# A one-core kernel with a written order: w_out in four transfers, in-place GpSimd additions, and a new order of all its steps

## The chip, the cores and the metric

The kernel runs on one NeuronCore of a Trainium2 chip. The metric is the device time of one execution in microseconds (us), as the median of several runs. A profile of one execution stands beside it; its times are counted from the start of its span, and the span is shorter than the device time by what lies around it.

The engines are named as the profile names them: PE is the matrix engine, PEld its weight loads, DVE the vector engine, ACT the scalar engine, POOL is GpSimd, and SP is the engine that issues nearly all transfers here.

## The reference

Two blocks follow each other. Attention has no softmax: queries and keys go through a sketch, and the values are gathered once per head.

```python
# q, k, v: (4, 4, 1088, 32); S1, S2: (8, 32), float64
a = einsum('rd,bhsd->bhsr', S1, x); b = einsum('rd,bhsd->bhsr', S2, x)
phi(x) = einsum('bhsi,bhsj->bhsij', a, b).reshape(..., 64)
kv = einsum('bhsf,bhsd->bhfd', phi(k), v);  z = sum(phi(k), axis=2)
x = (phi(q) @ kv) / (phi(q) @ z + 1e-6)        # back to (4352, 128)
# w1, w2: (128, 1024); w3: (1024, 1024); w_out: (1024, 128), float64
out = ((x @ w1) * (x @ w2)) @ w3 @ w_out       # (4352, 128)
```

The arithmetic is float32 on the chip. S1, S2 and the four weights arrive as float64, so the kernel reads their words as integers and builds float32 from them.

## The kernel before, in words

**Steps and their order.** All work is cut into 952 named steps. A step issues one or a few instructions, mostly on one engine. The string `ORDER` lists all of them, and the kernel calls them in that order (L1527); instructions of one engine are chained in it (L1530 to L1534), so `ORDER` fixes what each engine, and the queue of SP, does after what. An engine that waits holds back all that stands behind it. `SLOTS` fixes which buffer each tile takes, `POOL` and `ACTS` say which of the elementwise steps run on GpSimd or ACT rather than on DVE. The order was worked out outside the kernel; in the kernel it is a constant.

**Key side, one batch b of four.** `k{b}.load` and `k{b}.loadr` bring keys, `k{b}.max` and `k{b}.g` find their size, `k{b}.lead` and `k{b}.rest` split them in a leading and a small part, and `k{b}.gram0` to `gram4` (L604) multiply keys with keys in 144 small matmul passes of 32 columns by 128 rows. `Gm` to `Ts` and `N0`, `N1` shape the denominator; `ab`, `kp`, `kv0` to `kv3`, `kvr` and `kq` build phi(k) and kv.

**Query side.** `q0` to `q4`, `q6` and `qr` are seven groups of tokens, which fill the nine token tiles of the next block. In each, `tr`, `max`, `l2`, `l1`, `rm` split the queries, `A0`, `C0`, `C1` (L1294) project them, a run of DVE and GpSimd steps from `sm` to `phi` forms phi(q), `pT` turns it, and `x` (L1408) and `xT` (L1419) give the token tile of the next block.

**The feed-forward part.** For each token tile g (0 to 7 of 512 tokens, r of 256) and each of eight column blocks c there are five steps: `g{g}.{c}a` and `b` (L1448, L1458), one float32 matmul of two passes each; `c`, a copy by ACT (L1453); `m`, the product by DVE (L1464); and `o` (L1471), which accumulates the output. `w3` and `w_out` are multiplied into one matrix first: `f{n}.t` transposes a chunk of w3 on DVE (L472), and `f{n}.m` multiplies it with w_out in 16 passes on PE (L478).

**Weights.** `w0` and `w1` carry w1 and w2, `w2` carries w_out, `w3` to `w10` the eight chunks of w3. Each has a load, two readings of its words on ACT (`c` L229, `m` L417), a shift on DVE (`j` L431) and two integer additions on POOL (`a0`, `a1`). w_out comes in one transfer in which partition p holds rows 8p to 8p+7 (L396). The rows of w_out and the columns of w3 must be in one order, so for w3 the shift writes back into its own input and the two additions write the permuted order into another tile (L439 to L442).

**Fillers.** `warm0` to `warm28` are 72 matmuls on zeros whose results nobody reads (L221). They keep PE active in the places that the order gives them; there are as many of them after the change as before.

A step's *tile shape* is the part of the PE array that its passes use: 128x128 for the feed-forward part, 128x32, 64x32 or 32x32 for most of the attention part.

## Time and profile before

The median is 254.46 us of three runs (254.37 to 256.15). The profiled execution took 254.37 us; its span is 252.6 us, so 1.8 us lie around it. The granted clock of PE is 1.00 in all the stages below. PE works from 1.0 to 249.4 us; the first feed-forward matmul, `g0.3a`, starts at 30.3 us. The busy times are those of the profile's stage view, in us.

| Stage, us | PE | DVE | ACT | POOL | mean DMA share |
|---|---|---|---|---|---|
| 0 to 30.3, start | 28.02 | 24.43 | 19.21 | 15.43 | 0.71 |
| 30.3 to 60 | 29.67 | 27.25 | 21.34 | 14.81 | 0.88 |
| 60 to 95 | 35.00 | 33.52 | 21.50 | 14.91 | 0.72 |
| 95 to 120 | 24.01 | 17.05 | 7.27 | 9.45 | 0.08 |
| 120 to 165 | 45.00 | 30.56 | 14.64 | 10.51 | 0.01 |
| 165 to 249.4 | 84.40 | 26.92 | 15.78 | 1.71 | 0.16 |
| 249.4 to 252.6, tail | 0.01 | 0.29 | 0.00 | 0.00 | 0.20 |

Matmuls overlap in their pipeline, so a PE that is busy throughout can still lose time between two groups: then the next group starts later after the one before it than the passes alone need. That is read from the start times in the timeline, and not from the busy time.

### The profile page before, as it was taken

How to read it: one execution, taken by the hardware profiler on the slowest of the kernel's cores; microseconds unless marked ns; L12 is line 12 of the kernel's file. 1: busy time of each engine (PE TensorE's matmuls, PEld its weight loads, DVE VectorE, ACT ScalarE, POOL GpSimd, SP SyncE). 2: the span in 40 equal slices, each digit the busy share in tenths (PEclk: the TensorE clock that was granted, in tenths of full speed). 3: DMA queues.
4: the chain of work that ended last, by engine and by line, in shares of the span. 5: the costliest groups of instructions: out<-in, count | busy, mean ns of one | idle time of the engine just before them, and what ended most of it. 6: DMA issues, size and time to landing. Idle time of an engine off the chain costs nothing.

```text
span 252.6 us, 5980 instructions
## 1 busy us (share of the span) xinstructions
PE 246.1 (97%) x2503; PEld 137.9 (55%) x2503; DVE 160.0 (63%) x358; ACT 99.7 (39%) x183; POOL 66.8 (26%) x99
## 2 busy tenths in 40 slices
PE   8799999999999999998999999999999999999994
PEld 6689845457456576456446444444444444456554
DVE  2999998989998995938677597550115371424040
ACT  4588398763918543340225143213340012211010
POOL 4644535393546309203540016010000001000000
PEclk9999999999999999999999999999999999999999
DMA  6867793996679930200000000000000007205014
GB/s 182 262 173 263 222 241 84 259 254 139 160 206 235 249 90 0 85 6 3 3 0 3 3 0 1 4 0 0 3 0 0 0 2 123 44 0 83 0 28 76
DMA packets 31130, 22.01 MB, mean 87 GB/s; under 512 B 21248, under 2 KB 25600, under 8 KB 30976
## 3 DMA queue, kind: packets, MB, share of 16 engines
q1 hardware_dynamic: 30416, 21.05, 33.9%
q10 hardware_dynamic: 688, 0.59, 0.7%
q8 instruction: 19, 0.31, 0.5%
q14 instruction: 7, 0.06, 0.1%
HBM read 19.40 MB, written 2.23 MB: 86 GB/s over the span
## 4 chain that ended last, share of the span: by engine, by line
PE 95%; issue 1%; DMA 1%; POOL 1%; ACT 1%; DVE 0%; SPq 0%; POOLq 0%; ACTq 0%
PE a_ps L1448 23%; PE b_ps L1458 23%; PE ps_o L1471 22%; PE ps_w3o L478 6%; PE ps_g L604 3%; PE ps_x L1408 2%; PE idle_ps L221 2%; PE ps_ac L1294 2%; PE ps_kv L714 2%; PE ps_or L1478 1%; DMA s_raw<-in_S_dram 1%; PE ps_ab L672 1%; PE ps_ab L647 1%; PE ps_xt L1195 1%; PE ps_kt L630 1%
## 5 line engine op out<-in xcount | busy, mean ns | idle before, releaser
L1464 DVE TENSOR_TENSOR ab<-ffa,b_ps 128x512 f32<-128x512 f32 (+1 forms) x72 | 44.9, 649 | 60.8 <-PE b_ps L1458 40.9
L1453 ACT COPY ffa<-a_ps 128x512 f32<-128x512 f32 (+1 forms) x72 | 38.6, 566 | 96.4 <-PE a_ps L1448 93.8
L1448 PE MATMUL a_ps<-xT,w 128*128 128x512 f32 (+1 forms) x144 | 66.7, 570 | 0.0
L1458 PE MATMUL b_ps<-xT,w 128*128 128x512 f32 (+1 forms) x144 | 65.5, 569 | 0.0
L1471 PE MATMUL ps_o<-ab,w3o 128*128 128x512 f32 x128 | 62.3, 594 | 0.0
L1448 PEld LDWEIGHTS a_ps<-xT,w 128*128 128x128 f32 x144 | 26.5, 190 | 30.0 <-issue 23.9
L1458 PEld LDWEIGHTS b_ps<-xT,w 128*128 128x128 f32 x144 | 26.9, 190 | 29.1 <-issue 25.0
L1471 PEld LDWEIGHTS ps_o<-ab,w3o 128*128 128x128 f32 x128 | 23.9, 190 | 25.5 <-issue 24.0
L442 POOL TENSOR_TENSOR w3c<-cv_c,cv_m 128x512 int32<-128x512 int32 x16 | 20.8, 1333 | 22.0 <-DVE cv_c L431 13.7
L1389 POOL TENSOR_TENSOR ph<-s_al,s_bs 128x1024 f32<-128x1024 f32 (+1 forms) x6 | 10.8, 1808 | 52.7 <-DVE s_bs L1379 52.7
L478 PEld LDWEIGHTS ps_w3o<-wo,w3T 128*128 128x128 f32 x128 | 15.4, 192 | 3.6 <-issue 3.3
L478 PE MATMUL ps_w3o<-wo,w3T 128*128 128x128 f32 x128 | 15.6, 275 | 0.0
L221 PE MATMUL idle_ps<-zeros 128*128 128x256 bf16 x72 | 13.3, 317 | 1.0 <-DVE zeros L193 1.0
L229 ACT ACTIVATE cv_c<-raw 128x1024 f32<-128x1024 f32 x11 | 12.8, 1175 | 2.1 <-DMA raw<-in_moe_w_dram 2.1
L417 ACT ACTIVATE cv_m<-raw 128x1024 int32<-128x1024 uint32 x11 | 12.8, 1178 | 0.0
L472 DVE STREAM_TRANSPOSE w3T<-w3c 128x1024 f32<-128x1024 f32 x8 | 9.8, 1230 | 3.5 <-POOL w3c L442 3.5
L604 PE MATMUL ps_g<-kk 128*32 128x64 f32 x288 | 8.2, 225 | 2.1 <-POOL kk L596 1.1
L1346 POOL TENSOR_TENSOR s_al<-s_hl 128x128 f32<-128x128 f32 (+2 forms) x3 | 2.3, 753 | 29.7 <-DVE s_hl L1341 29.7
L1419 ACT COPY xT<-ps_x 128x128 f32<-128x128 f32 (+2 forms) x20 | 4.6, 325 | 13.1 <-PE ps_x L1408 9.5
L1397 DVE STREAM_TRANSPOSE pT<-ph 128x1024 f32<-128x1024 f32 (+1 forms) x7 | 8.2, 1164 | 2.5 <-POOL ph L1389 2.4
L221 PEld LDWEIGHTS <-zeros 128*128 128x128 bf16 x72 | 7.5, 114 | 3.9 <-issue 1.0
L604 PEld LDWEIGHTS ps_g<-kk 128*32 128x32 f32 x288 | 7.0, 109 | 2.8 <-POOL kk L596 1.2
(241 smaller groups left out, 284.3 us busy)
## 6 DMA issues: line engine op xcount, KB each, us to landing
raw<-in_moe_w_dram SPq DMA_DIRECT2D x32, 256.0 KB, 7.6
qh<-in_q_dram SPq DMA_DIRECT2D x4, 544.0 KB, 3.5
out_dram<-oT SPq DMA_DIRECT2D x33, 64.0 KB, 2.0
raw<-in_moe_w_dram SPq DMA_DIRECT2D x4, 512.0 KB, 5.8
k<-in_k_dram SPq DMA_DIRECT2D x3, 512.0 KB, 5.9
v<-in_v_dram SPq DMA_DIRECT2D x2, 512.0 KB, 6.4
raw<-in_moe_w_out_dram SPq DMA_DIRECT2D x1, 1024.0 KB, 6.0
kh<-in_k_dram SPq DMA_DIRECT2D x8, 128.0 KB, 6.3
```

The costliest lines, as they stand in the source:

```text
L221: pe.matmul(t, zeros, bview(zeros, [[0, 2], [1, 128]]), start=True, stop=True)
L229: act.activation(dst, hi.bitcast(F32), ACT.Prelu, scale=2.0 ** -112, alpha=-2.0 ** 32)
L417: act.mul(x["m"], words(0).bitcast(U32), 2.0 ** -29)
L442: pool.tensor_tensor(d, c, m, ALU.add)
L478: pe.matmul(t["o"], w3T[ko][:, c], wo[:, c], start=c == 0, stop=c == NC - 1)
L604: pe.matmul(o[h * D:(h + 1) * D], lhs, rhs, start=start, stop=stop, skip_group_check=True)
L1389: on(nm(f"phi{u}")).tensor_mul(x, bview(s["al"][:, u * g], [[r, g], [1, r], [0, r]]), bview(s["bs"][:, u * g], [[r, g], [0, r], [1, r]]))
L1448: pe.matmul(x["a"][:, :w], w_of(0, c), xT[g][:, c0:c0 + w], start=True, stop=True)
L1453: act.copy(x["s"][:, :w], x["a"][:, :w])
L1458: pe.matmul(x["b"][:, :w], w_of(1, c), xT[g][:, c0:c0 + w], start=True, stop=True)
L1464: dve.tensor_mul(ab_sb[g, c][:, c0:c0 + w], x["s"][:, :w], x["b"][:, :w])
L1471: pe.matmul(o_ps[g], w3o[:, c], ab_sb[g, c], start=c == 0, stop=c == NC - 1)
```

## The change

There are three edits; the third is by far the largest.

```diff
 w2.load:
-  sp.dma_start(raw[n], bass.AP(w_out, ap=[[NC * DM, 128], [1, NC * DM]]))
+  for t in QUARTERS:                       # 0, 2, 1, 3
+      sp.dma_start(raw[n][t * 32:(t + 1) * 32],
+                   bass.AP(w_out, offset + t * 256 * DM, ap=[[DM, 32], [32 * DM, NC], [1, DM]]))
 w{n}.j:
-  d = x["c"].bitcast(I32) if 3 <= n and n - 3 not in BY_PE else made()
-  on(f"w{n}.j").tensor_scalar(d, x["c"].bitcast(I32), 3, None, ALU.logical_shift_left)
+  on(f"w{n}.j").tensor_scalar(made(), x["c"].bitcast(I32), 3, None, ALU.logical_shift_left)
 w{n}.a0, a1:
-  if 3 <= n and n - 3 not in BY_PE:
-      (d, c, m as views with the two inner axes of d exchanged)
-      pool.tensor_tensor(d, c, m, ALU.add)
-      return
   d = x["d"].bitcast(I32)[:, i * 512:(i + 1) * 512]
   pool.tensor_tensor(d, d, x["m"][:, i * 512:(i + 1) * 512], ALU.add)
```

w_out now comes in four transfers of 32 partitions, each row of 1 KB on its own, so that partition p of part t holds rows 256t + 32c + p. With that, the columns of w3 need no permutation: the shift writes straight into the tile of the result, and both additions work in place and contiguously.

`ORDER`, `SLOTS`, `POOL` and `ACTS` are all replaced. The same 952 steps remain, with the same 2503 PE passes, so a step only moves. What the moves amount to, counted in the two orders:

- 25 elementwise steps change engine. From POOL to DVE: `s.low`, `s.sum`, `k0.rest0`, `s.blkh`, `q1.al`, `q1.p2`, `k1.kp1`, `q2.al`, `q4.phi0`, `q4.phi1`, `q6.p12`, `q6.phi1`, `qr.al`, `qr.p2`, `qr.phi0`. From DVE to POOL: `k0.kp1`, `q0.al`, `k0.Nf`, `k1.kp0`, `q3.p12`, `k3.rest0`, `q6.al`, `qr.p12`. From ACT to DVE: `s.lead`, `k3.lead0`.
- SP issues `k0.loadr` ahead of `s.load` (before: behind it). `c.act`, a copy of one element that came first on ACT, now stands far behind, after `g2.1c`.
- From `g0.3a` on, two neighbouring PE steps differ in tile shape in 42 places (before: 46), and 7 filler matmuls stand there (before: 10).
- `k2.kv0` to `kvr` and `k3.gram0` to `gram4`, which followed each other with `k3.ab` between them (232 passes), are now apart: the 144 passes of `k3.gram` come first, then seven feed-forward steps and a filler, then the 72 of `k2.kv`. `k2.gram0` to `gram4`, which had feed-forward and other steps close to them and `q1.x` among them, now come in one piece.
- At the end, the eight second halves of the last output (`gr.*o1`) come before the last four of the first halves; before, the first halves were through first.

## The prediction

> **What bounds the kernel now.** I read the page's busy shares and slices first, then PE's waits, then the chain in order of time, then the timeline of PE and the rows of the steps that move.

> ```profile
> span 252.6 us, 5980 instructions
> ...
> PE 246.1 (97%) x2503; PEld 137.9 (55%) x2503; DVE 160.0 (63%) x358; ACT 99.7 (39%) x183; POOL 66.8 (26%) x99
> ...
> PE   8799999999999999998999999999999999999994
> ...
> DVE  2999998989998995938677597550115371424040
> ...
> q8 instruction: 19, 0.31, 0.5%
> ```

> PE is the bound, and its 2503 passes stay. DVE's average of 63% hides that it stands at 8 or 9 in nearly every slice of 6.3 us up to 101 us. Queue q8 brought 0.31 MB of instructions in 19 packets: 16 KB each, about one per 125 passes.

> PE's own waits, then the chain in order of time around the longest of them after the start:

> ```profile
> PE ps_g L604 <- POOL kk L596: 1.1, 1, 1.1
> PE idle_ps L221 <- DVE zeros L193: 1.0, 1, 1.0
> PE ps_g L604 <- issue: 1.0, 1, 1.0
> PE ps_st L306 <- POOL sk_x L297: 0.2, 1, 0.2
> ```

> ```profile
> 113.97 1.03 PE ps_kv L714 x64
> 115.00 0.59 PE ps_ab L672 x16
> 115.85 1.64 PE ps_g L604 x79
> 117.48 0.99 issue
> 119.12 0.86 PE ps_o L1471 x2
> ```

> After the first 10 us PE stands idle for nothing but 0.99 us, and that wait has no releaser: the 232 short passes of `k2.kv`, `k3.ab` and `k3.gram` took some 3.5 us, one instruction packet started at 116.15, inside the gram, and PE went on at 118.48. I read it as instructions that came too late. What else PE loses is between shapes:

> ```profile
> 139.24 1.02 PE L1448 MATMUL a_ps<-xT,w 128*128 128x512 f32 x2
> 140.19 0.71 PE L1294 MATMUL ps_ac<-qT,RC 32*32 32x256 f32 x32
> 140.84 0.32 PE L1285 MATMUL ps_ac<-q,AR 64*32 64x256 bf16 x8
> 141.09 0.72 PE L1294 MATMUL ps_ac<-q,RC 32*32 32x256 f32 x32
> 141.74 0.44 PE L750 MATMUL ps_kq<-ident,kvc 128*128 128x128 f32 x2
> ```

> The first column is the start. Two passes of 512 columns follow the next pair after 0.86 us in the chain; here 0.95, so going over to 32x32 cost 0.09. Behind the last of the `x` steps the next matmul came up to 0.34 us late.

> **The change, part by part.** I count from 249.4, the end of PE's work, in three stretches: the start up to `g0.3a` (30.28 us before), PE's work from there on (219.1 us), and the tail (3.2 us).

> *The start.* DVE sets it: from `k0.max0` (5.63) to the end of `q0.xs` (28.70) it works nearly without a gap, and `q0.xs` leads through `q0.xt` and `q0.xT` to `g0.3a`. The sum of the DVE rows in that stretch is 22.9 us before. In the new order I add `k0.rest0` (0.70, from 128x512 tensor rows of 0.68), `s.pair` (0.74, now in this stretch), `s.lead`, `s.low`, `s.sum` and `s.blkh` (some 1.0 by rows of 0.17 to 0.28 of such size) and take off `k0.kp1` (1.16), `q0.al` (0.33), `k0.Nr` (0.09) and `k0.Nf` (0.10): 23.6. It can start earlier. `k0.max0` waited for `k0.loadr`, which was issued at 1.53 and landed at 5.51; the halves of the keys landed at 3.50 and 4.63. Issued at 0.74, `k0.loadr` should land with the second half, so I start at 4.7. `s.load` moves from 0.74 to 1.5 and so from a landing at 3.7 to some 4.4; with `c.act` gone from the front, the table load (1.28) now follows that landing, and `s.words` ends near 6.2, before DVE asks for it at 7.5. On POOL, `s.rest` and `k0.rest1` end near 11.2 (11.0 before), so `gram2` stays where it was. One new wait is visible: `q0.phi0` on DVE waits for `q0.al` on POOL, behind `kr0.kp`, `s.zero`, `Nh`, `Nf`: about 0.4. So `q0.xs` ends at 4.7 + 23.6 + 0.4 = 28.7, as before. `w0.a0`, which gated `g0.3a` in the trace (it ended at 30.05), ends near 29.2 now. `k1.ab` and `k0.kqt` still stand between: `g0.3a` at 30.1, **−0.2**, between −1.3 (no wait, 4.5 as start, and no fillers in the way) and +1.0 (`k0.loadr` lands as late as now).

> *PE's work from there.* Fillers: 10 to 7, at 0.11 each in the chain (0.87 for seven): **−0.3**. Shapes: four changes fewer, two of 128x32 to 32x32 (0.11 each in the starts) and two of 32x32 to 128x32 (0.34 and 0.10), against odd pairs that cancel: −0.4 by four times 0.09, −0.7 by their own prices; I take **−0.5**. The wait for instructions: the longest run of short passes falls from 232 to some 160 (`k2.gram` and `k1.N`), and the 144 of `k3.gram` are followed by seven long steps, 6 us. Before, 150 short passes from 61 to 64 us went without such a wait. So **−1.0**; the ends are −1.0 and 0.

> *DVE beside it.* By its rows it gains 4.7 us of work (165.0 to 169.7), most of it before 77 us. At `f2.m`, which stands at 76.4 on PE without stalls, the new order has put 71.6 us of DVE work ahead: 71.4 from 4.7 on ends at 76.1 if DVE never waits, 0.3 us of room. Where a PE step names a DVE result, I subtracted the sum up to that result from PE's own sum: the least room was 0.6 before (`k1.T1`) and is −0.3 now (`g0.0a` behind `k1.abt`), with four more below 0.5 up to 50 us. I take **+0.6**, between 0 and +2.

> *w_out, SP and the additions.* Whole, w_out landed 6.0 us after its issue; a w3 chunk in four parts issued from 72.57 landed by 80.5, so 8. SP issues three instructions more, some 1.3 us, ahead of `w3.load`. In the new order the issue waits for `k1.gram4` (about 24.6), two transfers of v1 stand before it, and it lands near 35; `w2.m` is the first to read it, at about 42, with `q2.l2` and `q1.xT` queued behind it on ACT. That is 7 us of cover, and 0 is the cost; without it each us late would hold `q1.xT` and with it `g1.2a`. The strided additions took 1333 ns, the contiguous ones 1274 and, for w_out, 1640: 16 of them save 0.9 us of POOL or lose 4.9, over 60 us in which POOL is half idle. 0.

> *Tail.* `gr.oT0` on ACT is now the last copy in place of `gr.oT1` on DVE (0.27 and 0.29), and a transfer from ACT follows. `g6.st` can go 2.5 us before PE's end and takes 1.9 of SP. 0, within 0.1.

> Sum: −0.2 − 0.3 − 0.5 − 1.0 + 0.6 = −1.4. The span goes to 251.2, the profiled execution to 253.0, and, 0.1 above it as before, the median to **253.1 us**.

> **The rivals.**

> *DVE becomes the bound between 30 and 95 us.* In the trace DVE lost, beside its late start, 2.0 us in waits up to 75.9. If it loses them again, and its rows are 3% longer because more of them stand beside POOL (71.6 x 0.03 = 2.1), it reaches `f2.m` 4.1 − 0.3 = 3.8 us late, and PE, whose order allows no other step, with it. In place of +0.6 that is +3.8: −2.0 + 3.8 = +1.8, 256.3 us. It decides from 2.3 us of lost DVE time on, and ends slower than before. For it: the load, and that the moves to POOL (`k1.kp0`, `k3.rest0`, `q3.p12`) make DVE wait for a slower engine. Against it: the same kind of order held with 0.6 us of room. Chance 0.21.

> *The wait for instructions stays.* 144 short passes take 1.7 us, less than the 2.3 from the packet's start to PE's return; if a packet boundary falls badly, the gram stalls as before, or `k2.gram` does. Then −0.4: 254.1 us. Chance 0.20. [...]

> *The start gains what DVE's earlier start offers.* If the waits in it vanish and `g0.3a` comes at 28.9, and DVE keeps ahead later, the sum is −1.4 − 1.2 − 0.6 = −3.2: 251.3 us. For it: `w0.a0` no longer gates. Against it: `k1.ab`, `k0.kqt` and 23.6 us of DVE rows. Chance 0.19.

> **How the numbers follow.** My forecast has 0.40. The range goes from the third rival's 251.3, less 0.5 for the start's lower bound, to the first one's 256.3: 250.8 to 256.3, which leaves out about 0.2. One per cent of 254.46 is 2.5 us, about what a measurement here can tell from no change, so faster is below 251.9 and slower above 257.0. Faster: most of the third rival (0.15) and a share of the forecast (0.10), 0.25. Slower: 0.08 of the first rival and 0.07 for a stall I have not seen, 0.15. The rest, 0.60, lies within 1%.

> **What would show it.** Right: no PE wait without a releaser behind `ps_g`; `k0.max0` near 4.7 and `g0.3a` near 30; between 30 and 95 us PE waits of some 0.6 us in all, behind DVE. Wrong: DVE at 9 throughout with PE waiting on `ab`, `xT` or a transposed tile; a gap in `ps_g`; ACT standing before `cv_m` for w_out's last quarter; a tail over 3.3 us.

## The result and the profile after

| | before | after |
|---|---|---|
| median, us | 255.31 (254.37 to 256.58) | 262.33 (260.37 to 263.11) |
| runs | 4 | 4 |
| profiled execution, us | 254.37 | 262.17 |
| its span, us | 252.6 | 260.4 |

The ratio is 1.0272, with an interval of 1.0232 to 1.0312: the changed kernel is 2.7% slower. The forecast was 253.1, and its range ended at 256.3.

The page of the changed kernel: busy time, two of the engines' rows in forty slices of 6.5 us, the granted clock, and the instruction queue. (Line numbers of this file are up to 8 lower than those of the kernel before, and those of the files below differ again by a few.)

```profile
span 260.4 us, 5986 instructions
...
PE 248.1 (95%) x2503; PEld 139.4 (54%) x2503; DVE 174.1 (67%) x368; ACT 95.5 (37%) x177; POOL 62.4 (24%) x92
...
PE   8989999789999999999999999999999999999990
...
DVE  3988999988999989999987856422335820333320
...
PEclk9999999979999999999999999999999999999996
...
q8 instruction: 19, 0.31, 0.5%
```

The passes and the instruction packets are the same. DVE is busy 14.1 us longer, and POOL 4.4 us less. PE has a hole in the eighth slice (45.6 to 52.1 us) and the ninth, the clock falls in the ninth, and the last slice is empty. All of PE's waits that the view lists:

```profile
PE ps_ac L1277 <- DVE AR L346: 2.8, 1, 2.8
PE ps_kv L713 <- DMA v<-in_v_dram: 1.1, 1, 1.1
PE idle_ps L220 <- DVE zeros L192: 1.0, 1, 1.0
PE ps_N L854 <- DVE T_p L842: 0.5, 1, 0.5
```

The wait of 1.0 behind `ps_g` that had no releaser is gone. In its place stands one of 2.8 behind DVE, for `s.AR` at `q2.A0`. PE and DVE alone don't explain it; with POOL beside them the timeline does (start, duration, engine, line):

```profile
49.28 1.94 POOL L614 TENSOR_TENSOR kp<-kabt 128x1024 f32<-128x1024 f32 x1
...
50.28 2.20 DVE L880 TENSOR_TENSOR AR<-RC,mask2n 128x16 bf16<-128x16 f32 x1
...
51.18 1.26 POOL L437 TENSOR_TENSOR wo<-wo,cv_m 128x512 int32<-128x512 int32 x1
...
52.40 0.68 DVE L1264 SCALAR_TENSOR_TENSOR q<-q,qT 128x512 f32<-128x512 bf16 x1
...
53.00 0.21 DVE L346 TENSOR_TENSOR AR<-Sc,mask2n 128x64 bf16<-128x64 f32 x1
...
53.27 0.25 PE L1277 MATMUL ps_ac<-q,AR 64*32 64x128 bf16 x8 [2.81 <-DVE AR L346]
```

`k1.Nr` on DVE (L880) multiplies 16 elements per partition. Elsewhere it takes 0.17 us; here it takes 2.20 and ends with the second of two POOL instructions, `k1.kp0` and `w2.a1`. `q2.rm`, `s.AR` and then PE stand behind it.

Less than 1 us after its pause PE runs at half clock. Stretches of one microsecond; the number ahead of the DMA share is the granted clock:

```profile
53.00:54.00 1.00, 0.73 (x41) 0.47 (x41) 1.00 (x3) 0.65 (x1) 0.00 (x0) 1.00 0.92 219
54.00:55.00 1.00, 1.00 (x2) 0.49 (x3) 0.97 (x4) 0.00 (x0) 0.00 (x0) 0.53 1.07 390
55.00:56.00 1.00, 1.00 (x2) 0.47 (x2) 1.00 (x6) 0.00 (x0) 0.00 (x0) 0.50 1.03 205
56.00:57.00 1.00, 1.00 (x2) 0.34 (x1) 0.76 (x3) 0.00 (x0) 0.00 (x0) 0.50 1.04 234
57.00:58.00 1.00, 1.00 (x3) 0.41 (x2) 0.34 (x1) 0.00 (x0) 0.00 (x0) 0.77 1.07 238
```

The half clock lasts 3.4 us. `g1.5b` and `g1.7b` take 1.75 and 1.71 us there, in place of 0.86 each: +1.74. PE counts as busy while it happens (1.00 of each stretch from 54.00 on), so no wait shows it.

The tail, in the timeline of SP's and ACT's queues and in SP's waits:

```profile
250.91 6.32 SPq L1418 DMA_DIRECT2D out_dram<-oT  x4
...
253.81 0.64 ACTq L1424 DMA_DIRECT2D out_dram<-oT  x1
257.33 0.61 SPq L1424 DMA_DIRECT2D out_dram<-oT  x1
```

```profile
SPq L1418 <- DMA out_dram<-oT: 4.6, 1, 4.6
```

The four transfers of `g6.st` took 6.32 us to issue; before, the same four took 1.95. The first went at 250.91, the second 4.6 us after the end of the first, at 255.83, and `gr.st1` behind them at 257.33. From PE's end to the end of the span it is 6.9 us, before 3.2.

The sum of the two profiles, in spans (+7.8): the start +0.6 (`g0.3a` begins at 30.9, before at 30.3); the wait at `q2.A0` +2.9; the half clock +1.7; a later wait at `k3.N1` +0.9; the tail +3.7; and, as what remains, −2.0 in the rest of PE's work. (The two waits are taken from start times, by which they cost somewhat more than the 2.8 and 0.5 us of idle time in the list.) From `g0.3a` to PE's end it is 222.6 us, before 219.1.

A median below is over all runs of a kernel, while its ratio and interval compare its fast runs alone with fast runs of the kernel before from the same session, and three profiles (`tail_sp`, `one_sbuf` and `k1_first`) are of slow runs, so that only single durations are read from them.

### The profile page after: what moved, and what is told of

Same layout as the page of the kernel before. It is cut to its first block, busy times and chain, and to the rows that moved or that the text cites. A ratio compares the mean times of both kernels' runs of the same rounds, so it can differ in the third digit from the quotient of the medians.

```text
span 260.4 us, 5986 instructions
## 1 busy us (share of the span) xinstructions
PE 248.1 (95%) x2503; PEld 139.4 (54%) x2503; DVE 174.1 (67%) x368; ACT 95.5 (37%) x177; POOL 62.4 (24%) x92
## 4 chain that ended last, share of the span: by engine, by line
PE 75%; DVE 11%; issue 5%; POOL 4%; DMA 2%; SPq 1%; ACT 1%; POOLq 0%
PE b_ps L1450 19%; PE a_ps L1440 19%; PE ps_o L1463 18%; PE ps_w3o L470 3%; PE idle_ps L220 3%; DVE ab L1456 2%; DMA v<-in_v_dram 2%; PE ps_ac L1286 2%; DVE kp L614 1%; POOL kk L588 1%; PE ps_or L1470 1%; PE ps_x L1400 1%; PE ps_g L596 1%; POOL w3c L437 1%; DVE ph L1381 1%
## 5 line engine op out<-in xcount | busy, mean ns | idle before, releaser
L1450 PE MATMUL b_ps<-xT,w 128*128 128x512 f32 (+1 forms) x144 | 69.0, 584 | 0.0
L1440 PE MATMUL a_ps<-xT,w 128*128 128x512 f32 (+1 forms) x144 | 66.0, 572 | 0.0
L1440 PEld LDWEIGHTS a_ps<-xT,w 128*128 128x128 f32 x144 | 26.7, 191 | 30.9 <-issue 26.0
L1463 PEld LDWEIGHTS ps_o<-ab,w3o 128*128 128x128 f32 x128 | 23.6, 190 | 22.4 <-issue 20.7
L437 POOL TENSOR_TENSOR w3c<-w3c,cv_m 128x512 int32<-128x512 int32 x16 | 20.3, 1294 | 13.9 <-DVE w3c L431 8.4
L1479 DVE STREAM_TRANSPOSE oT<-ps_o 128x512 f32<-128x512 f32 x8 | 5.7, 710 | 19.5 <-PE ps_o L1463 19.5
L470 PEld LDWEIGHTS ps_w3o<-wo,w3T 128*128 128x128 f32 x128 | 15.2, 192 | 2.9 <-issue 1.9
L418 ACT ACTIVATE cv_m<-raw 128x1024 int32<-128x1024 uint32 x11 | 12.9, 1185 | 0.0
L1352 POOL TENSOR_TENSOR s_pr<-s_pr 128x128 f32<-128x128 f32 (+2 forms) x4 | 2.0, 490 | 32.1 <-DVE s_pr L1348 31.6
L614 POOL TENSOR_TENSOR kp<-kabt 128x1024 f32<-128x1024 f32 x3 | 5.8, 1945 | 10.2 <-DVE kabt L682 10.2
L1338 POOL TENSOR_TENSOR s_al<-s_hl 128x256 f32<-128x256 f32 x2 | 2.4, 1223 | 22.7 <-DVE s_hl L1333 22.7
## 6 DMA issues: line engine op xcount, KB each, us to landing
raw<-in_moe_w_dram SPq DMA_DIRECT2D x32, 256.0 KB, 6.3
raw<-in_moe_w_out_dram SPq DMA_DIRECT2D x4, 256.0 KB, 5.9
```

Source lines behind the costliest of these rows:

```text
L418: act.mul(x["m"], words(0).bitcast(U32), 2.0 ** -29)
L437: pool.tensor_tensor(d, d, x["m"][:, i * 512:(i + 1) * 512], ALU.add)
L470: pe.matmul(t["o"], w3T[ko][:, c], wo[:, c], start=c == 0, stop=c == NC - 1)
L614: eng.tensor_mul(dst, bview(av, [list(av.ap[1]), list(av.ap[2]), [0, r]]), bview(bv, [list(bv.ap[1]), [0, r], list(bv.ap[2])]))
L1440: pe.matmul(x["a"][:, :w], w_of(0, c), xT[g][:, c0:c0 + w], start=True, stop=True)
L1450: pe.matmul(x["b"][:, :w], w_of(1, c), xT[g][:, c0:c0 + w], start=True, stop=True)
```

## The experiments

**The edits without the new order.** Is it the transfers and the additions, or the order? `edits_only` keeps the order, the engines and all else of before and takes the two edits of code alone.

> Kernel before, its order and engines kept, with the first two edits alone: w_out in four transfers and the additions in place (the buffer of each w3 tile is taken at the shift instead of at the first addition). Theory (all of the loss lies in the new order): no change, 254.2 to 255.2 beside 254.6, PE's waits as before (0.99 us behind ps_g, no other after 12 us). Rival (the edits themselves cost, because a transfer in 1 KB rows lands later or an in-place addition holds DVE longer): over 256, with a PE wait of 1 us or more between 30 and 80 us.

Measured: 255.04 us, ratio 1.0016 (0.9994 to 1.0038). Under the old order, the transfers of w_out and the in-place additions cost nothing that can be measured. Everything that follows is about the new order.

**What holds DVE.** `probe` appends small DVE instructions behind the last step, first alone and then each beside a POOL instruction. They are extra work, so this kernel's own time says nothing.

```diff
+ add  = pool.tensor_tensor(W3, W3, WO, ALU.add)        # in place, 128x512
+ stt  = dve.scalar_tensor_tensor(N8, U, 2.0, V, ...)   # two SBUF inputs, 128x32
+ both = dve.tensor_add(N8, U, V)                       # two SBUF inputs
+ psum_in = dve.tensor_add(N8, psum, V)                 # one input in PSUM
+ scal = dve.tensor_scalar(N8, U, col, col, ...)        # one SBUF input and a column
```

> Changed kernel with test instructions behind its last step, on tiles that nobody needs any more; its time is longer by these and means nothing. DVE instructions on 128x32 run alone and then beside a POOL instruction that started first. Theory (held DVE): a sum of two SBUF tensors (with scalar_tensor_tensor or tensor_tensor) takes 0.1 to 0.2 us alone and 0.6 to 1.2 us beside an integer addition of 128x512 on POOL, ending within 0.05 us of POOL's end, whether that addition is in place or strided, and beside a float product too; a sum with one input in PSUM, a sum and difference with a column, a reduction, a transpose and a copy stay as they are alone. Rival (POOL does not hold DVE): every DVE instruction takes the same alone and beside POOL, within 0.05 us. Open: a copy and a memset on POOL.

The timeline of the probe; the first two rows are alone, the others beside a POOL addition:

```profile
260.89 0.18 DVE L1527 TENSOR_TENSOR RS<-x_p,RS 128x32 f32<-128x32 f32 x1
261.11 0.30 DVE L1528 TENSOR_SCALAR RS<-RS,KS 128x32 f32<-128x32 f32 x1
...
263.36 1.26 POOL L1516 TENSOR_TENSOR w3o<-w3o,wo 128x512 int32<-128x512 int32 x1 [76.93 <-DVE w L1532]
263.55 1.11 DVE L1524 SCALAR_TENSOR_TENSOR RS<-RS 128x32 f32<-128x32 f32 x1
...
265.95 1.26 POOL L1516 TENSOR_TENSOR w3o<-w3o,wo 128x512 int32<-128x512 int32 x1 [1.33 <-DVE wo L1532]
266.21 1.05 DVE L1525 TENSOR_TENSOR RS<-RS 128x32 f32<-128x32 f32 x1
...
271.13 1.26 POOL L1516 TENSOR_TENSOR w3o<-w3o,wo 128x512 int32<-128x512 int32 x1 [1.33 <-DVE wo L1532]
271.39 0.18 DVE L1527 TENSOR_TENSOR RS<-x_p,RS 128x32 f32<-128x32 f32 x1
271.61 0.82 DVE L1528 TENSOR_SCALAR RS<-RS,KS 128x32 f32<-128x32 f32 x1
```

The forms with two SBUF inputs take 0.18 alone and 1.05 to 1.11 beside the addition, and each ends within 0.05 us of POOL's end. One input in PSUM: 0.18 in both. One SBUF input with a column from SBUF: 0.30 alone, 0.82 beside, and here the forecast, that it would stay as it is alone, missed. Beside a strided POOL addition of 1.91 us the two-input form took 1.85, beside a POOL copy (1.04) 0.90, beside a memset (0.96) 0.18. The probe's reduction, transpose and copy came behind the 0.82 and started when POOL was through, so they tell nothing; the kernel's own transposes of 128x1024 take 1.20 to 1.25 beside POOL and without it.

The trace of the changed kernel shows one thing more: the 2.20 us of `k1.Nr` went on past the end of `k1.kp0` (51.22) to the end of `w2.a1` (52.44), so DVE did not go on between these two POOL instructions, of which the second started at 51.18.

**Other forms on DVE.** `one_sbuf` writes the steps that suffered with one tensor input: `G_a` and `N` from PSUM, and `Nr` with a column.

```diff
- dve.tensor_mul(AR[:, b, :, 1], bview(RC[:, b, 1, 1], ...), bview(mask2n, ...))
+ for i in range(2):
+     dve.tensor_scalar(AR[:, b, i, 1], RC[:, b, 1, 1], mask2n[:, i:i + 1], None, ALU.mult)
```

> Changed kernel with three small groups of DVE instructions in another form, so that none of them reads two tensors from SBUF: G_a and the first part of N each as one addition and subtraction of a column straight from PSUM, AR of k.Nr as two products with a column of the mask. Theory (held DVE: a DVE instruction with both inputs in SBUF that starts while a POOL instruction works waits for that one's end): G_a (1.27 us), RC (0.98 and 0.64) and AR (2.20) return to 0.2 or less, DVE is 3.5 to 4 us earlier at q2.A0, PE's wait of 2.8 us there falls below 0.5, the half clock behind it (1.7 us lost) does not come, and the median falls by 3.5 to 5 us, to 257.3 to 258.8. Rival (DVE is simply overloaded by its 4.7 us of added work): the instructions are long for another reason or others take their place, PE waits at least 2 us, the median stays within 1 us of 262.3.

Measured: 265.2 us (two runs at 260.9 and 262.7, two at 267.7 and 267.8), ratio 1.0277 (1.0236 to 1.0319): a miss. PE's wait at `q2.A0` was 2.9, as before. Its timeline shows the two `Nr` instructions held as the one was (they are one row, x2):

```profile
53.59 3.53 DVE L880 TENSOR_SCALAR AR<-RC,mask2n 128x8 bf16<-128x8 f32 x2
...
53.90 1.95 POOL L614 TENSOR_TENSOR kp<-kabt 128x1024 f32<-128x1024 f32 x1
...
55.81 1.27 POOL L437 TENSOR_TENSOR wo<-wo,cv_m 128x512 int32<-128x512 int32 x1
```

The probe's 0.82 says why: this form, a tensor and a column both in SBUF, is held too. Whether the column does it or the form itself was not tested apart. The forms with the tensor in PSUM and a column in SBUF took 0.28 beside POOL, so these two steps were mended, and the decisive one was not.

**Is the half clock a second cost of the pause?** `filled` puts one filler of 24 matmuls into it.

```diff
- s.AR g1.7a g1.1c q2.C0 w3.a1 w3.a0 f0.t q2.A0
+ s.AR g1.7a g1.1c q2.C0 warm29 w3.a1 w3.a0 f0.t q2.A0
```

> Changed kernel with 24 filler matmuls (2.6 us) between q2.C0 and q2.A0, where PE stood idle for 2.8 us. Theory (PE's pause costs twice): the granted clock stays at full in the 4 us behind q2.A0, the pairs there take 0.86 us instead of 1.75, and the median falls by 1.7 us to 260.6, with PE's step q2.A0 still at 53 us. Rival (the clock drop has nothing to do with the pause, or the fillers come in the way): no change or up to 0.3 us slower.

The same stretches in `filled`:

```profile
54.00:55.00 1.00, 1.00 (x41) 0.56 (x36) 1.00 (x2) 0.24 (x1) 0.00 (x0) 1.00 0.99 198
55.00:56.00 1.00, 1.00 (x4) 0.46 (x3) 0.97 (x5) 0.00 (x0) 0.00 (x0) 1.00 1.00 386
```

The clock stays at 1.00, both pairs take 0.86 again, and from `g0.3a` to PE's end it is 221.3 us in place of 222.6. The time, 261.23 (ratio 1.0278, 1.0229 to 1.0327), shows no gain that one could tell; the span of its profile is 259.5. DVE's wait itself stayed, as it must.

**Is the tail a wait of SP for ACT's late transfer?** `tail_sp` issues the last half but one from SP, and last.

```diff
- gr.oT1 gr.st0 g6.st gr.st1
+ gr.oT1 g6.st gr.st1 gr.st0
- (sp if u else act).dma_start(out ...)
+ sp.dma_start(out ...)
```

> Changed kernel with one edit: both short stores of the last 256 tokens go out on SP's queue, behind g6.st, as g6.st, gr.st1, gr.st0 (before: gr.st0 on ACT's queue). Theory (shared counters): the second transfer of g6.st waits for a completion counter that gr.st0 holds, and gr.st0 can only start when PE is through. Then SP's 4.6 us between 251.2 and 255.8 us vanish, the last issue ends near 254.4 instead of 257.9, the tail behind PE's last matmul goes from 6.9 to some 3.2 us, and the median falls from 262.3 to about 258.7. Rival (the transfers themselves are slow, eight of 512 short packets each stand in line): the wait stays, one more issue on SP, 262.3 to 263.

SP's queue at the end of `tail_sp`:

```profile
255.10 1.95 SPq L1418 DMA_DIRECT2D out_dram<-oT  x4
257.14 1.44 SPq L1424 DMA_DIRECT2D out_dram<-oT  x2
```

The issues take 1.95 again, the wait of 4.6 is gone, and from PE's end to the end it is 3.3 us in place of 6.9. The time is 260.51 (1.0198, 1.0155 to 1.0241), 1.8 below the changed kernel where 3.6 were expected; its runs lie between 258.3 and 263.86 us, and in the profile the start is 3 us later than in the changed kernel (`g0.3a` at 33.9). Which landing SP waited for stands in the trace of the changed kernel: `gr.st0`, which ACT issues only when PE is through (253.81), landed at 255.82, and 0.01 us later SP issued the second part of `g6.st`. In that trace the transfers of SP and ACT name eight semaphores for their completion, 14 or 15 transfers each; `gr.st0` and that second part both name 110, and the second part also waits for 110. In the trace of the kernel before `gr.st0` names 102, and only the wait at the end of the program (250.50) names 102 after it.

**The start.** In the new order `k1.load` is issued at 4.81, behind `kr0.load` (before: 3.59). `k1_first` puts it ahead.

```diff
- k1.loadr kr0.load kr0.tr ... s.tc kr0.kT ... warm13 k1.load
+ k1.loadr k1.load kr0.load ... s.tc ... warm13 kr0.tr ... k0.kT0 kr0.kT
```

> Changed kernel with k1.load issued ahead of kr0.load on SP's queue, as in the kernel before, and kr0.tr and kr0.kT put behind s.R and k0.kT0. Theory (the start hangs on k1.load): k1.max starts by 11.0 us in every profile (10.96 to 12.80 in the four of this order so far), k_g is over before POOL starts k0.kp1, g0.3a comes at 29.9 to 30.6 us (31.0 to 34.6 so far), and the median falls by 0.7 to 2 us with a smaller spread between runs. Rival (start set by v0 or by DVE's sum): g0.3a stays at 31 or later, the median within 0.5 us.

Measured: 262.18 us (259.6 to 266.04), ratio 1.0255 (1.0187 to 1.0323): a miss, no gain alone, and its runs lie 6.4 us apart. In its profile `g0.3a` comes at 34.9, behind two waits without a releaser, 1.3 and 2.6 us, and 3.4 us of half clock. The next runs, which hold the same edit, are closer together.

**Start and tail together.** `start_tail` is `k1_first` with the edit of `tail_sp`.

> Changed kernel with two repairs, k1.load first (k1_first) and the last stores all on SP (tail_sp), nothing else. Theory (the two are independent, and the start of k1_first depends on when instruction packets and loads get their turn on the loaded DMA engines): 3.7 us less than k1_first whatever the start does, so 255.9 at the fastest run and a spread of some us between runs. Rival (the order of k1.load alone settles the start): a spread below 1.5 us, and g0.3a between 29.5 and 30.5 us as in all_fixed and best, with 256.5 to 258.

Measured: 258.52 us (257.43 to 258.98), ratio 1.0147 (1.0126 to 1.0169), `g0.3a` at 30.4, tail 3.4. The wait of 2.8 at `q2.A0`, the half clock and the wait at `k3.N1` (0.85) are as they were. Here the rival came nearer than the theory: the runs lie 1.6 us apart and `g0.3a` is where it put it, though the time is above its 256.5 to 258. The time is 3.95 us above that of before in its session (254.57), the changed kernel 7.0 above that in its own (255.31; in the later sessions it was 254.4 to 255.0), so start and tail account for 3.1 or somewhat more; by the two profiles it is 4.0, 0.5 in the start and 3.5 in the tail.

**Keep POOL off `k1.Nr`.** `gated` lets the additions wait for `s.AR`, by a POOL copy that reads its result.

```diff
- w3.j w2.a0 ... s.AR g1.7a g1.1c q2.C0 w3.a1 w3.a0 f0.t q2.A0
+ w3.j ... s.AR x.gate w3.a1 w3.a0 w2.a0 g1.7a g1.1c q2.C0 f0.t q2.A0
+ x.gate: pool.tensor_copy(t, AR[:1, 1, 0, 0])
```

> Changed kernel with one more POOL instruction, a copy of 8 values of AR behind s.AR, and the POOL additions w3.a1, w3.a0 and w2.a0 placed behind it, so that they can only start when DVE is through with k2.Ga, k1.Na, k1.Nr, q2.rm and s.AR. No DVE instruction is changed. Theory (held DVE): G_a, RC and AR between 40 and 54 us take 0.2 us or less each (1.27, 0.98 and 2.20 before), PE's wait of 2.8 us at q2.A0 falls below 0.7, no half clock behind it, the median falls by 3.5 to 4.5 us to 258 to 259. Rival (DVE is overloaded, the long instructions only replace waiting): the wait stays above 2 us and the median within 1 us of 262.

`k2.Ga`, `k1.Nr` and `s.AR` took 0.22 us or less, PE took `q2.A0` without a wait, and the clock stayed full there. But the hold only moved; the timeline of `gated` behind it:

```profile
56.29 1.94 POOL L619 TENSOR_TENSOR kp<-kabt 128x1024 f32<-128x1024 f32 x1
...
57.82 1.92 DVE L166 SCALAR_TENSOR_TENSOR s_t<-s_g,ay_A 128x256 f32<-128x256 f32 x1
...
58.19 1.25 POOL L442 TENSOR_TENSOR wo<-wo,cv_m 128x512 int32<-128x512 int32 x1
```

The delayed `k1.kp0` and `w2.a1` now hold `s_t` (0.42 elsewhere), and `f0.t` on DVE waited 2.74 for the additions; PE waited 1.5 at `g1.3a` and 0.7 at `q3.C0`. The time was 262.74 (261.21 to 265.5; 1.0291, 1.022 to 1.0362): no gain. The profile is of a run of 264.24 us with a start 2.4 us later than in the changed kernel (`g0.3a` at 33.2): `k0.kvr` had waited 2.2, and the clock was 0.50 for 3.4 us from 19.9 on.

**All of it.** `all_fixed` is `start_tail` with the gate, and with `k3.Ts` ahead of `k3.abt`, so that the step that `k3.N1` needs is not behind a held `k3.kp1`.

> Changed kernel with four repairs together: k1.load first (k1_first), POOL's additions behind AR (gated), k3.Ts ahead of k3.abt so that PE's k3.N1 does not wait behind k3.kp1, and the last stores all on SP (tail_sp). Theory (these four places hold the whole loss): waits of PE after 12 us below 1.0 us in all, tail 3.2 us, 252 to 253.5, faster than the kernel before by 0.5 to 1%. Rival (other instructions are held in their place, for DVE has 4.7 us more work): 255 to 258, with a new PE wait behind DVE between 50 and 95 us.

Measured: 256.17 us, ratio 1.0057 (1.0036 to 1.0079): 2.35 below `start_tail`, but not below the kernel before. The wait at `k3.N1` is gone; 1.5 at `g1.3a` and 0.7 at `q3.C0` remain, both behind DVE.

**Is the wait behind `ps_g` worth 1 us?** `split` is the kernel before with three long steps between its short passes.

```diff
- k2.kvr k3.gram0 ... k3.Gm g0.4o g2.5a ... g2.5m g3.6b
+ k2.kvr g0.4o g2.5a g3.6b k3.gram0 ... k3.Gm ... g2.5m
```

> Kernel before with one move: the feed-forward steps g0.4o, g2.5a and g3.6b (2.6 us of long passes) go from behind k3.gram4 and k2.kqt to ahead of k3.gram0, so that the run of 232 short passes falls into 88 and 144. Theory (PE waited for instructions): the 0.99 us (1.2 in edits_only) behind ps_g vanish and nothing takes their place, the median falls by 0.8 to 1.0 us to about 253.7. Rival (the wait has another cause, or the next packet is as late at the new place): a wait of about 1 us stays behind ps_g or shows elsewhere, 254.4 to 255.

The complete list of PE's waits in `split`, without the two that were there before:

```profile
PE a_ps L1441 <- DVE ab L1457: 0.8, 1, 0.8
```

The wait without a releaser is gone, so it did hang on the long run of short passes; but PE, now earlier at `g2.5a`, waits 0.8 for DVE. 255.31 us, ratio 1.0006 (0.9985 to 1.0027): no gain. That PE waited for instructions is borne out by the traces side by side: in the kernel before, `edits_only`, `start_tail`, `k1_first`, `vr_best3`, `one_sbuf` and `probe` PE has eight waits of 0.18 to 2.56 us without a releaser, and each ended 1.3 to 1.6 us after the end of an instruction packet (before: the packet that started at 116.15 ended at 117.09, and PE went on at 118.47).

**Can the new order be made to win?** `best` takes `k1.kp0` back to DVE and puts the additions where DVE has no two-input steps; `best2` moves `f0.t`, `w2.a0` and `w4.j` once more; `best3` moves four products and `k2.Tb` earlier on DVE. All three hold the edits of `start_tail`, and `k3.Ts`.

```diff
 best:  - w3.j ... s.AR ... k1.kp0 (POOL)      + s.AR k1.kp0 (DVE) w3.j w2.j w3.a1 w3.a0 ... q2.sh f0.t ... q2.p12 w2.a0 w2.a1
 best2: - q2.sh f0.t; g1.5a w4.j; w2.a0 w2.a1  + q3.l1 f0.t ... q2.sh; g1.5m w4.j; w3.a0 w2.a0 ... w2.a1
 best3: + g1.1m, g0.5m g1.0m, g0.4m, k2.Tb earlier
```

> Changed kernel with the start and tail of all_fixed and k3.Ts ahead of k3.abt, and another cure for the held instructions in place of the gate: k1.kp0 goes back from POOL to DVE, and on DVE k1.kp0, w3.j and w2.j stand behind s.AR, so that POOL has no addition to make before; f0.t stands behind q2.sh, w2.a0 and w2.a1 behind q2.p12. Theory (held DVE): of the waits that all_fixed still has (1.5 us at g1.3a, 0.7 at q3.C0, some 0.3 behind it) less than 0.7 us is left, PE needs 218 to 219 us from g0.3a to its end (all_fixed 221.1, before 219.1), 252.5 to 254 us, below the kernel before. Rival (DVE's added work): DVE's backlog shows at another place between 50 and 95 us with 1.5 us or more, 255 to 257.

> The kernel called best with three more moves: f0.t on DVE ahead of q2.sh instead of behind it, w2.a0 on POOL directly behind w3.a0 (POOL was idle there from 54.1 to 59.1 us), and w4.j on DVE behind g1.5m, so that the products that free q3.C0's banks come 0.7 us earlier. Theory (held DVE; in best four held instructions between 53 and 65 us took 2.35 us too long, and PE waited 2.45 us more than its passes need at q3.C0 and g0.2b): PE's waits there fall below 1.2 us in all, PE needs 218.5 to 219.5 us from g0.3a to its end (best 220.4, before 219.1), and the median falls by 1 to 2 us to 254 to 255. Rival (DVE's own work sets the pace there): the same wait shows up at g0.2b or one step later, 255.5 or more.

> The kernel called best2 with the order of DVE changed between 55 and 65 us alone: the products g1.1m, g0.5m, g1.0m and g0.4m, each with one input in PSUM, come as soon as their matmuls are through (g1.1m directly behind g1.7m, g0.5m and g1.0m behind g1.0b, g0.4m behind g1.5m), ahead of the q2 group's chain, and k2.Tb directly behind k2.Ta. DVE does the same work. Theory (what best2 still loses, 2.7 us at q3.C0, g1.6a and g0.2b, is DVE's order: a bank is freed by a product that stands behind work that nobody waits for yet): less than 0.8 us of that is left, PE needs 218 to 218.6 us from g0.3a to its end (best2 220.3, before 219.1), the median falls by 1.5 to 2.2 us to 253.2 to 253.9, below the kernel before. Rival (DVE's sum of work is too much for these 70 us, whatever its order): the q2 group's results come later by what the products gain, PE waits the same 2 us or more at q2.x0 or at f0.m to f1.m, and the median stays above 255.

Measured: `best` 255.85 (1.0029, 1.0007 to 1.005), `best2` 255.33 (1.0027, 1.0013 to 1.0041), `best3` 255.98 (1.0054, 1.0036 to 1.0072). All three forecasts missed; `best` and `best3` landed where their rivals put them, `best2` between the two. `best2` is 3.2 us below `start_tail`: it has neither a pause of 2.8 nor a half clock, yet PE still waits behind DVE. Its list, without the fillers at the start:

```profile
PE b_ps L1443 <- DVE ab L1449: 0.9, 1, 0.9
PE a_ps L1433 <- DVE T_p L821: 0.3, 1, 0.3
PE ps_ac L1279 <- DVE ab L1449: 0.2, 1, 0.2
```

From `g0.3a` to PE's end it is 220.3 us in `best2` and 220.1 in `best3`, against 222.4 in `start_tail` and 219.1 before. In its profile `best3` loses at the start and not behind it: `g0.3a` comes at 30.3, in `best2` at 29.5, and `k0.kvr` waited 0.8 for the last rows of the values.

**What sets the start.** That wait stands in the changed kernel, too. Its chain of waits (start, duration):

```profile
13.26 0.61 SPq L545
13.92 4.93 DMA v<-in_v_dram
18.86 0.14 issue
18.99 0.32 PE ps_kv L713 x8
```

`v0.loadr`, 32 KB, is issued at 13.92 and lands 4.9 us later; from there to `g0.3a` PE has no gap. Before, the transfer was issued at 14.44 and landed at 18.4, and `k0.kvr` began at 20.2. The new order has `k0.kvr` some 2.5 us earlier on PE, were it not for the wait (`k0.kv0` begins at 16.8, and `k0.kvr` can follow 0.9 later). Three runs issue the transfer behind `v0.load`, 1.3 us earlier: `vr_start` from `start_tail`, `vr_best2` and `vr_best3` from the two others.

```diff
- v0.load k0.kp0 ... s.zero kr1.load v0.loadr q0.C0t
+ v0.load v0.loadr k0.kp0 ... s.zero kr1.load q0.C0t
```

> Edit: start_tail with v0.loadr (32 KB, the last rows of the values of batch 0) issued right behind v0.load, ahead of kr1.load, on SP. My theory of the start: in the new order PE's steps k0.kv stand 2 us earlier than before (16.6 instead of 18.3 us), so k0.kvr, which was covered before (19.98, landing 18.4), now waits for v0.loadr, which is issued at 13.9 and lands 2.7 to 6.2 us later. From k0.kvr to g0.3a there are 11.8 us without a gap in most profiles. Issued 1.3 us earlier it lands near 16.6 and k0.kvr comes some 0.5 us earlier than in start_tail (17.8): g0.3a near 29.8 instead of 30.4 (by the instructions' mean start, 29.5 to 29.7 by the other count), time near 258.0, and runs closer together. Rival A: something else sets the start (DVE's rows up to q0.xs): g0.3a and the time stay, 258.5. Rival B: kr1.load, now 0.6 us later, lands at 17.6 and becomes the new gate at kr1.tr: no gain or a loss of up to 0.5 us.

> Edit: best2 with v0.loadr behind v0.load, as in vr_start. In best2's profile k0.kvr was held by 0.31 us only. Theory: g0.3a 0.3 us earlier, time 255.0 (best2 255.33). Rival A: no change, 255.3. Rival B: kr1 as the new gate: 255.3 to 255.8.

> Edit: best3 with v0.loadr behind v0.load. In best3's profile k0.kvr was held by 0.96 us, while from g0.3a to PE's end best3 took 220.07 against 220.30 in best2. Theory: what best3 lost (255.98 against 255.33) was the landing of this transfer and not its order; with it out of the way 254.9 to 255.1, not above vr_best2. Rival: the order of best3 itself is worse in most runs (DVE's work at another place): time 255.6 to 256.0, above vr_best2 by 0.4 or more, with the PE time from g0.3a on over 220.5.

(The starts of PE's steps that these expectations name are counted from 0.24 us into the span.) In all three `k0.kvr` follows 0.67 us behind `k0.kv3`, without a wait. `vr_start`: `g0.3a` at 29.7 (30.4 in `start_tail`), 257.9 us, ratio 1.0139 (1.0115 to 1.0163). Of its 0.73 us only 0.24 is this wait (`k0.kvr` began 1.16 behind `k0.kv0` in `start_tail`, 0.92 in `vr_start`); 0.34 was there before it, since `k0.gram3` already began 0.36 earlier, and 0.15 came behind it. `vr_best2`: 255.99, 1.0049 (1.0032 to 1.0065); in its profile `k0.gram3` began 1.1 us later than in that of `best2`, and `g0.3a` came at 30.4 (29.5 in `best2`). `vr_best3`: 255.62, 1.0028 (1.0008 to 1.0049), 220.1 from `g0.3a` on. Its `g0.3a` came at 30.3, as in `best3`: PE now waited 0.5 for keys (`kr0`) and 0.5 without a releaser. So the order of `best3` is no worse than that of `best2`, what it gains from `g0.3a` on is 0.2 us, and the start is set by several landings that differ from run to run, of which this is one. No kernel of the experiments beat the kernel before.

## Why the prediction was wrong

The forecast was −1.4 us, the profiles show +7.8. Three steps failed, here by their place: the start (0.8 off), "DVE beside it" (4.9) and the tail (3.7).

**The start, −0.2, was +0.6.** The step that failed is "DVE sets it". DVE did start early, at 4.06 (4.7 was forecast), and ended `q0.xs` at 29.0; but the chain runs over `v0.loadr`, a transfer that I did not move in my head because the change moves only its reader. Its cover had been 1.8 us (20.2 less 18.4). PE waited 1.1 for it and had no gap from there to `g0.3a`; without the wait `g0.3a` would have come near 29.7. The three runs with an earlier issue show that the wait goes with it; the start went with it in `vr_start` alone, and there only in part.

**Fillers, shapes and instructions, −1.8: −2.0 in the profile.** The −2.0 is what remains of a sum, so it bears out the three terms together; of the single ones only the wait, −1.0, is seen by itself. That wait is gone in the changed kernel, and in `split` it goes when the run of short passes is broken, against the rival that it stays. What `split` and the mended versions add: without that wait PE waited behind DVE, 0.8 us in `split` (ratio 1.0006) and 0.9 in `best2`.

**"DVE beside it", +0.6 between 0 and +2, was +5.5:** 2.9 for the wait, 1.7 for the clock and 0.9 at `k3.N1`. This step failed in its method. I summed DVE's durations from the trace of before, in which they stand beside other POOL work, and priced a nearer POOL at 3% of DVE's rows in the rival, an estimate that was worked out from no row. The rows did not grow by a share: `k1.Nr`, 0.17 us elsewhere, grew to 2.20, up to the end of the POOL work beside it. By the rows of nine such instructions after, each less the shortest row of its form, 10.6 us were lost, most in an `s_pr` of 2.90 in place of 0.43 and in `k1.Nr`; before, 1.2 us in four. The difference and the 4.7 us of added work make up the 14.1 us that DVE is busy longer. The trace of before showed the pattern, with `T_p` at 0.48 in place of 0.18, and I did not ask what those four had in common. The rival that ends slower had the right engine and the right waits ("PE waiting on `ab`, `xT` or a transposed tile" was the sign, and `s.AR` is another); but its price of +3.8 and its mechanism, a loss spread over many rows, were not what happened, and the half clock was in no rival. The 5.5 us say where the time went, and not what a mend of these places returns: from `start_tail` to `best2`, without this wait, the half clock and the one at `k3.N1`, PE's work after `g0.3a` fell by 2.1 us only (222.4 to 220.3), and other waits behind DVE came up.

**The tail, 0 within 0.1, was +3.7.** I counted that `g6.st` "takes 1.9 of SP" and that it could go 2.5 us before PE's end. It could, but for its second part, which waited for a transfer that ACT issues after PE's end. The step looked at queues and data, not at the landing that the issue waited for (255.82). `tail_sp` and every run that holds its edit show 3.3 to 3.4.

**w_out and the additions, 0, were right**: `edits_only` measured 1.0016. The four transfers were issued between 25.9 and 28.7, each landed 5.4 to 6.0 us later, where 8 were allowed, and ACT read w_out without a wait for them.

Put together, the forecast's sum with the measured DVE term in place of its own, −2.0 + 5.5, gives 254.5 + 3.5 = 258.0 us; `start_tail`, in which start and tail are mended, measured 258.52. That says that the parts add up; it is no test of each.

What stays open: why the runs of `k1_first` lie 6.4 us apart and those of `gated` 4.3, and those of the kernels with both edits of `start_tail` at most 1.8 (the profiles of `k1_first`, `gated`, `tail_sp` and `one_sbuf` all have a stretch of half clock in the start, behind waits that the other profiles lack); and what keeps `best2` 1.2 us behind the kernel before from `g0.3a` to PE's end. It can be the amount of DVE's work (4.7 us more by its rows), its order, or the hold itself, which `best2` did not do away with: by the same count its DVE rows still lose 8.9 us, 4.1 of it between 30 and 95 us, where the changed kernel lost about 6. Whether this order could win without any hold was not tested.

## What to carry to other kernels

When an order is changed, list for each DVE instruction with two SBUF inputs which POOL instructions can stand beside it. In the probe such an instruction, 0.18 us alone, took 1.05 to 1.11 beside an addition of 1.26 and 0.90 beside a copy of 1.04, but 0.18 beside a memset: its price was the rest of the POOL work, not its own duration. One that PE waits for was better placed ahead of POOL's work (`k1.Nr` took 0.22 or less in `gated`) or fed from PSUM (0.18 in the probe). A wait of PE has to be priced with the clock that follows it (here 2.8 us of waiting, and 3.4 us at half clock behind it), and a step that moves earlier on PE has to be checked against the landing of every transfer that it reads, the small ones too (32 KB held `k0.kvr` by 1.1 us). A late transfer on one queue can hold an unrelated one on another, here by 4.6 us, so look at SP's waits at the end before its count of instructions.

## What the runs showed of the hardware that was not expected

The hold seems to work the other way round, too, even for one tensor. In `best3` a DVE shift of one tensor started 0.02 us behind a POOL addition and took its usual 0.69, and POOL took 1.82 in place of 1.26:

```profile
61.18 1.82 POOL L430 TENSOR_TENSOR wo<-wo,cv_m 128x512 int32<-128x512 int32 x1
61.20 0.69 DVE L424 TENSOR_SCALAR w3c<-cv_c 128x1024 int32<-128x1024 int32 x1
```

In the profile of `k1_first` PE stood for 1.3 and 2.6 us in the start. Two packets of its instructions came late: they started at 12.9 and 19.7 us, when PE had already begun 433 and 705 matmuls and weight loads; in `all_fixed`, with the same start, they started at 10.9 and 15.2, after 265 and 512. Full DMA engines do not explain both: they were 0.10 to 0.34 busy in the 2.1 us ahead of the first packet, and 0.82 to 0.97 in the 3.4 us ahead of the second. The cause is open; no run tested it.
